# A decode kernel on one core: w2 in small early transfers, fewer VectorE instructions, wo's first half in wide matmuls

## The chip, the cores and the metric

The kernel runs on one core of a Trainium2 chip. A core has five engines that run at the same time, each through its own list of instructions: TensorE (PE; its weight loads are shown apart as PEld), VectorE (DVE), ScalarE (ACT), GpSimd (POOL) and SyncE (SP). Here SyncE does nothing but issue transfers. Sixteen DMA engines move data between the chip's main memory and the core's on-chip memory. Engines wait for each other through semaphores. The metric is the device time of one execution in microseconds (us), lower is better. It is given as the median of the runs shown.

## The reference

For a batch of two and one new token each, the result is a gated mix of attention against a long cache and a small feed-forward block (the reshapes are left out):

```python
g = sigmoid((x * gate_w).sum(-1))                 # x: [2, 512]
q = (x @ wq)                                      # 32 heads of 128
scores = einsum(q, k_cache) * 128 ** -0.5         # k_cache: [2, 32, 4096, 128], bf16
o = einsum(softmax(scores), v_cache)              # v_cache: the same size
a = o @ wo                                        # wo: [4096, 512]
b = relu(x @ w1) @ w2                             # w1: [512, 1376], w2: [1376, 512]
out = g * a + (1 - g) * b                         # [2, 512]
```

The two caches are 67.1 MB each. All input together is 145.4 MB, and every byte is read once.

## The kernel before

The program is written engine by engine. Each instruction is recorded with the markers it waits for and the marker it signals; `resolve` and `emit` (lines 57 to 82) turn them into semaphore counts. An engine runs its instructions in the order in which the program records them. A wait on more than one semaphore becomes an instruction of its own (line 76 or 78), and it counts as a record of the engine's program.

**Units and regions.** The K cache is cut into eight units K0 to K7 of 8 MB, and the V cache into V0 to V7. They pass through three regions of on-chip memory (`NREG`, the tensor `kv`), in the order K0 to K4, V0, K5, V1, K6, V2, K7, V3 to V7 (line 169). Unit number n goes into region n mod 3, and SyncE issues its transfer only when the unit three places earlier has been used up: a K unit when its scores are done (marker `pe_sc_u`), a V unit when its products are done (`pe_v_u`). So V1 waits for the scores of K4, and V0 for those of K2. SyncE's transfers all go through one queue (q1) in program order. V7 comes in two parts.

**A K unit.** VectorE transposes the unit in place (`k_turn`, line 360) in four instructions, one for each quarter of the columns. TensorE computes the scores (`k_scores`, lines 365 and 393) in four parts `rp`, 16 matmuls each, and part `rp` waits for transpose number `rp`. The scores of four units, one batch row, stand in the accumulation memory (PSUM) together. After K3 comes the softmax of the first batch row: `sm_max` (VectorE), `sm_exp` (ScalarE), and `sm_turn` (VectorE, line 422), and only behind it on VectorE's list comes the transposition of K4. After K7 comes the softmax of the second.

**A V unit.** GpSimd spreads the probabilities into `ptm` (line 431), TensorE multiplies (`v_unit`, line 448), VectorE picks out the wanted quarter and sums (`v_extract`, lines 455 and 459), and TensorE gathers (line 464). `o_denominator` forms 1 / sum for one batch row, `o_scale` applies it with the gate.

**The beginning.** x and gate_w come through ScalarE's queue, one row each per partition; `gate` transposes them on TensorE, VectorE copies and multiplies, and a matmul with ones sums up. `q_proj` and `ffn_h` (line 336: x @ w1 in 11 tiles, ten of 128 and one of 96) follow.

**The end.** wo and w2 go into the region that V5 has left (marker `pe_v_5`), in this order: two halves of wo (2 MB each), 96 rows of w2 (w2a), then 640 (w2b, 5 KB a partition), 512 (w2c, 4 KB) and 128 (w2d, 1 KB). `o_place` lays the attention result out as weights `oW`. `project` (line 500) multiplies in 32 steps of wo and 11 of w2; each step is four matmuls of 128 columns, side by side on four column groups of TensorE, with two columns of weights each. Four small casts and one transfer give the output.

Of the kernel before, what the change touches and what calls it, by code (L numbers as in the profile page):

```python
# [4 lines left out]
ALU = mybir.AluOpType  # L5
ACT = mybir.ActivationFunctionType
AX = mybir.AxisListType
# [3 lines left out]
DFF = 1376  # L11
# [73 lines left out]
def bass_gated_mix__gqa_block_cached__dense_activation_relu__decode_kernel(  # L85
# [22 lines left out]
    id2 = sb("id2", [2, 2], bf16)  # L108
    xT = sb("xT", [128, 4, 2], bf16)
    xT32 = sb("xT32", [128, 4, 32], bf16)  # L110
    gwT = sb("gwT", [128, 4], bf16)
    xg = sb("xg", [128, 4, 2], f32)
    xgs = sb("xgs", [128, 2], f32)
# [17 lines left out]
    oW = sb("oW", [128, 32, 2], bf16)  # L131
    hT = sb("hT", [128, 11, 2], bf16)
# [8 lines left out]
    x_sb = kv[0:2, C, 21888:22400]  # L141
    gw_sb = kv[0:1, C, 22400:22912]
    ident = kv[:, C, 22912:23168].bitcast(f32)
    ones = kv[:, C, 23168:23424].bitcast(f32)
# [19 lines left out]
    names = ["x", "gw", "wq", "w1", "v7a", "v7b", "wo0", "wo1", "w2a", "w2b", "w2c", "w2d", "cast", "out"]  # L164
# [47 lines left out]
    w2_sb = kv[:, WO, 16384:22016].rearrange("p (r n) -> p r n", n=512)  # L212

    act(lambda e: e.dma_start(x_sb, A_x.rearrange("b s d -> (b s) d")).then_inc(sem["x"], 16))
    act(lambda e: e.dma_start(gw_sb, gate_w.rearrange("(o d) -> o d", o=1)).then_inc(sem["gw"], 16))
    sp(lambda e: e.dma_start(wq_sb, A_wq.rearrange("(p t) n -> p (t n)", t=4)).then_inc(sem["wq"], 16))
    sp(lambda e: e.dma_start(w1_sb, B_w1.rearrange("(p t) f -> p (t f)", t=4)).then_inc(sem["w1"], 16))
    for n, what in enumerate(order):
        if n >= NREG:
            waits = [freed(order[n - NREG])]  # L220
        else:
            waits = ["pe_h", "dve_setup", "dve_q"] if n == C else []
        if what == ("v", 7):
            sp(lambda e, n=n: e.dma_start(kv[:, n % NREG, 0:LASTV * 128], unit_in(("v", 7))[:, 0:LASTV * 128])
               .then_inc(sem["v7a"], 16), waits=waits)
            sp(lambda e, n=n: e.dma_start(kv[:, n % NREG, LASTV * 128:REG], unit_in(("v", 7))[:, LASTV * 128:REG])
               .then_inc(sem["v7b"], 16))
        else:
            sp(lambda e, n=n, what=what: e.dma_start(kv[:, n % NREG, :], unit_in(what)).then_inc(sem_reg[n % NREG], 16),
               waits=waits)  # L230
    for x in range(2):
        sp(lambda e, x=x: e.dma_start(wo_sb[:, x * 8192:(x + 1) * 8192],  # L232
                                      A_wo[x * 2048:(x + 1) * 2048, :].rearrange("(p r) n -> p (r n)", p=128))
           .then_inc(sem[f"wo{x}"], 16), waits=([freed(order[wo_reg - NREG])] if x == 0 else []))

    sp(lambda e: e.dma_start(w2_sb[0:96, 10, :], B_w2[1280:1376, :]).then_inc(sem["w2a"], 16))
    W2 = (("w2b", 0, 5, 0), ("w2c", 640, 4, 5), ("w2d", 1152, 1, 9))
    for name, row, n, r0 in W2:
# [7 lines left out]
    def constants():  # L246
        pool(lambda g: g.memset(id2[:], 0.0), signal="c_idz")
        pool(lambda g: g.affine_select(out=id2[:], in_=id2[:], pattern=[[-1, 2]], compare_op=ALU.not_equal, fill=1.0,
                                       base=0, channel_multiplier=1), waits=["c_idz"], signal="c_id2")
        pool(lambda g: g.memset(ones, 1.0), signal="c_ones")  # L250
# [3 lines left out]
        pool(lambda g: g.memset(xT32[:], 0.0), signal="c_x32")  # L254
        for i in range(2):
            pool(lambda g, i=i: g.memset(wz[:, i], 0.0), signal=("c_wz" if i else None))
        pool(lambda g: g.memset(mpad[:], 0.0), signal="c_mpad")
        pool(lambda g: g.memset(selx[:], 0.0), signal="c_selx")
# [6 lines left out]
    def setup():  # L265
        dve(lambda v: v.tensor_reduce(out=maskc[:], in_=ident.rearrange("p (t c h) -> p c t h", t=4, c=4), axis=AX.XY, op=ALU.add),
            waits=["c_ident"])
        dve(lambda v: v.tensor_reduce(out=mmax[:], in_=ident.rearrange("p (h x) -> p h x", h=8), axis=AX.X, op=ALU.add),
            signal="dve_m8")
        dve(lambda v: v.tensor_copy(out=mask8[:], in_=mmax[:]), waits=["dve_m8"], signal="dve_mask8")  # L270
# [8 lines left out]
    def gate():  # L279
        for t in range(4):  # L280
            pe(lambda e, t=t: e.transpose(PSB[0:128, XT_B0 + 2 * t:XT_B0 + 2 * t + 2], x_sb[:, t::4], id2[0:2, 0:2]),
               waits=(["c_id2"] if t == 0 else []), dwaits=([(sem["x"], 16)] if t == 0 else []))
        for t in range(4):
            pe(lambda e, t=t: e.transpose(PSB[0:128, XT_B0 + 8 + 2 * t:XT_B0 + 9 + 2 * t], gw_sb[:, t::4], id2[0:1, 0:1]),  # L284
               dwaits=([(sem["gw"], 16)] if t == 0 else []), signal=("pe_xT" if t == 3 else None))
        dve(lambda v: v.tensor_copy(out=xT[:], in_=PSB[0:128, XT_B0:XT_B0 + 8].rearrange("p (t b) -> p t b", t=4)),  # L286
            waits=["pe_xT"], signal="dve_xT0")
        dve(lambda v: v.tensor_copy(out=xT32[:, :, 0:2], in_=PSB[0:128, XT_B0:XT_B0 + 8].rearrange("p (t b) -> p t b", t=4)),
            waits=["c_x32"], signal="dve_x32")
        dve(lambda v: v.tensor_copy(out=gwT[:], in_=PSB[0:128, XT_B0 + 8:XT_B0 + 16:2]), signal="dve_xT")  # L290
        dve(lambda v: v.tensor_tensor(out=xg[:], in0=xT[:], in1=gwT[:].unsqueeze(2).to_broadcast([128, 4, 2]), op=ALU.mult),
            waits=["dve_xT"], signal="dve_xg")
        dve(lambda v: v.tensor_reduce(out=xgs[:], in_=xg[:].rearrange("p t b -> p b t"), axis=AX.X, op=ALU.add),
            waits=["dve_xg"], signal="dve_xgs")
        pe(lambda e: e.matmul(psf(0, 128, G_C0, 2), lhsT=ones, rhs=xgs[:, :], start=True, stop=True),
           waits=["dve_xgs", "c_ones"], signal="pe_z")
# [10 lines left out]
    def q_proj():  # L307
        wqv = wq_sb.rearrange("p (t u a x) -> p t a u x", t=4, u=4, a=4)
        for half in range(2):
            for t in range(4):  # L310
                for a in range(4):
# [4 lines left out]
                       waits=(["dve_xT0", "dve_x32"] if half == 0 and t == 0 and a == 0 else []),  # L316
# [9 lines left out]
    def ffn_h():  # L326
        for ft in range(11):
            m = 128 if ft < 10 else 96
            for t in range(4):
                def fn(e, ft=ft, t=t, m=m):  # L330
                    o = t * DFF
                    cols = w1_sb[:, o + 1280:o + 1376]
                    for _, row, n, r0 in W2:
                        if r0 <= ft < r0 + n:
                            cols = w1_sb[:, o + row + ft - r0:o + row + 128 * n:n]
                    return e.matmul(psf(0, m, H_C0 + 2 * ft, 2), lhsT=cols, rhs=xT[:, t, :], start=(t == 0), stop=(t == 3))
                pe(fn, dwaits=([(sem["w1"], 16)] if ft == 0 and t == 0 else []),
                   signal=("pe_h" if ft == 10 and t == 3 else None))
        for b in range(2):
            dve(lambda v, b=b: v.tensor_scalar(out=hT[:, 0:10, b], in0=PSF[:, H_C0 + b:H_C0 + 20:2], scalar1=0.0,  # L340
                                               scalar2=gm[:, b:b + 1], op0=ALU.max, op1=ALU.mult),
                waits=["pe_h", "dve_gm"])
            dve(lambda v, b=b: v.tensor_scalar(out=hT[0:96, 10, b:b + 1], in0=psf(0, 96, H_C0 + 20 + b, 1), scalar1=0.0,
                                               scalar2=gm[0:96, b:b + 1], op0=ALU.max, op1=ALU.mult),
                signal=f"dve_h{b}")
# [10 lines left out]
    def k_turn(u):  # L356
        what = ("k", u)
        reg = kv[:, reg_of(what), :].bitcast(dt.uint32)
        for rp in range(4):
            dve(lambda v, rp=rp: v.transpose(out=reg[:, 4096 * rp:4096 * (rp + 1)], in_=reg[:, 4096 * rp:4096 * (rp + 1)]),  # L360
                dwaits=([landed(what)] if rp == 0 else []), signal=f"dve_kt_{u}_{rp}")
# [8 lines left out]
    def k_scores(u):  # L370
        b, ub = divmod(u, 4)
        keys = kv[:, reg_of(("k", u)), :].rearrange("p (r j q e) -> p r j q e", j=2, q=32, e=2)
        for rp in range(4):
            pos = 8 * ub + 2 * rp
            for blk in range(4):
                j, e_ = divmod(blk, 2)
                for rb in range(4):
                    rc = 4 * rp + rb
                    waits = []
                    if blk == 0 and rb == 0:  # L380
                        waits = [f"dve_kt_{u}_{rp}"]
# [16 lines left out]
    def sm_max(b):  # L398
        dve(lambda v: v.tensor_reduce(out=mpad[:, 0:2], in_=PSF[:, 0:2048].rearrange("p (x h q) -> p h x q", h=2, q=16),  # L399
                                      axis=AX.XY, op=ALU.max),  # L400
            waits=[f"pe_sc_{4 * b + 3}", "c_mpad"] + ([f"dve_mt{b - 1}"] if b else []), signal=f"dve_m{b}")
# [51 lines left out]
    def v_extract(v):  # L453
# [4 lines left out]
            waits=[f"pe_v_{v}"] + ([f"dve_y_{v - 1}"] if v else []), signal=f"dve_x_{v}")  # L458
        dve(lambda e: e.tensor_reduce(out=X3[:], in_=X2[:].rearrange("p (c d) -> p d c", c=4), axis=AX.X, op=ALU.add),  # L459
            waits=[f"dve_x_{v}"] + ([f"pe_g_{v - 1}"] if v else []), signal=f"dve_y_{v}")  # L460
# [7 lines left out]
    def o_denominator(b):  # L468
        for h in range(2):
            pe(lambda e, h=h: e.matmul(psf(0, 32, L_C0 + b, 1), lhsT=sell[:, h, :], rhs=lsum[:, b, h:h + 1],  # L470
                                       start=(h == 0), stop=(h == 1), skip_group_check=True),
               waits=([f"act_exp{b}", "dve_setup", "dve_h1"] if h == 0 else []), signal=(f"pe_l{b}" if h else None))
        dve(lambda v: v.reciprocal(out=rinv[:, b:b + 1], in_=psf(0, 32, L_C0 + b, 1)), waits=[f"pe_l{b}"], signal=f"dve_rinv{b}")

    def o_scale(b):
        dve(lambda v: v.tensor_scalar(out=O_sb[:, b, :], in0=psf(0, 32, O_C0, 128), scalar1=rinv[:, b:b + 1],
                                      scalar2=gb[0:32, b:b + 1], op0=ALU.mult, op1=ALU.mult),
            waits=[f"pe_g_{4 * b + 3}", f"dve_rinv{b}", "dve_g"], signal=f"dve_O{b}")

    def o_place():  # L480
        for x in range(2):
            for dq in range(8):
# [6 lines left out]
        dve(lambda v: v.tensor_copy(out=oW[:].rearrange("p (x r) c -> p x r c", x=2),  # L489
                                    in_=psf(0, 128, R_C0, 64).rearrange("p (x b r) -> p x r b", x=2, b=2)),  # L490
            waits=["pe_R"], signal="dve_oW")


    def project():
        steps = [(oW[:, r, :], wo_sb[:, r * 512:(r + 1) * 512]) for r in range(32)]
        steps += [(hT[0:96, 10, :], w2_sb[0:96, 10, :])] + [(hT[:, r, :], w2_sb[:, r, :]) for r in range(10)]
        lands = {0: "wo0", 16: "wo1", 32: "w2a", 33: "w2b", 38: "w2c", 42: "w2d"}
# [92 lines left out]
```

## Time and profile before

| | |
|---|---|
| time, median of 3 runs | 344.62 us (344.28 to 344.64) |
| profiled execution | 344.46 us |
| its span, first to last instruction | 343.1 us |
| PE busy | 179.8 us (52%), 1322 instructions |
| DVE busy | 169.7 us (49%), 87 instructions |
| ACT, POOL busy | 13.5 us, 35.5 us |
| read from main memory | 145.43 MB, 424 GB/s over the span |
| q1, SyncE's transfers | 98.5% of the 16 engines' span |

The span runs from the first to the last instruction, so the profiled execution has 1.36 us around it. Times of day in the text ("at 145.06") count from the start of the span. The slices part of the page cuts the span into 40 equal pieces of 8.6 us and gives each engine's busy share in tenths. The chain of waits follows the work back from the last instruction: each line has a start, a length, and what ran or what was waited for. "issue" in it is time in which the engine waited for nothing that the profile shows. The time line has start, length, engine, line, operation and, in brackets, idle time before it and what ended that. Behind these views the trace also holds one record for each DMA packet (start, length, queue, bytes) and, for each transfer, the moments at which each of its engines reported its part as landed.

### The profile page before, as it was taken

To read this page: it belongs to the slowest core of one execution; us is meant where nothing else is said; L and a number is where in the kernel's file an instruction comes from. 1 tells how busy PE (TensorE), PEld (TensorE's weight loads), DVE (VectorE), ACT (ScalarE), POOL (GpSimd) and SP (SyncE) were. 2 spreads that over 40 slices of the span, in tenths; PEclk is the share of its full clock that TensorE was granted. 3 is DMA by queue.
4 is the path that set the end of the run, shared out by engine and by line. 5 is a ranking of instruction groups with operands and counts; after the bars stand their busy time and mean duration, and the time that the engine had idled before them with its cause. 6 is when DMAs were issued, how large, how long until landed. Compare 5 with 4: busy or idle time off the path is not lost.

```text
span 343.1 us, 2541 instructions
## 1 busy us (share of the span) xinstructions
PE 179.8 (52%) x1322; PEld 39.6 (12%) x938; DVE 169.7 (49%) x87; ACT 13.5 (4%) x44; POOL 35.5 (10%) x50
## 2 busy tenths in 40 slices
PE   0510196996869409935980099205970503307353
PEld 0210000100001000120120011100020201102122
DVE  0210797979899489439910694219935020102020
ACT  1010001000010110000000000000020000000000
POOL 3000000000000040040013000400004040403100
PEclk9965599899989957995995579955996575856586
DMA  8998989999999989898999989999999999999995
GB/s 325 451 483 374 481 374 481 397 458 420 435 460 390 489 382 474 382 468 390 466 466 391 481 384 466 405 451 405 460 405 443 466 392 474 413 401 449 395 428 216
DMA packets 3588, 145.59 MB, mean 424 GB/s; under 512 B 405, under 2 KB 634, under 8 KB 890
## 3 DMA queue, kind: packets, MB, share of 16 engines
q1 hardware_dynamic: 3572, 145.43, 98.5%
q8 instruction: 9, 0.15, 0.2%
q10 hardware_dynamic: 6, 0.00, 0.0%
q14 instruction: 1, 0.01, 0.0%
HBM read 145.43 MB, written 0.00 MB: 424 GB/s over the span
## 4 chain that ended last, share of the span: by engine, by line
DMA 57%; DVE 24%; PE 9%; issue 4%; another core or an unknown queue 3%; SPq 1%; ACT 1%
DMA kv<-in_A_k_cache_dram 34%; DVE kv L360 22%; DMA kv<-in_B_w_dram 13%; DMA kv<-in_A_v_cache_dram 11%; PE PS L365 4%; PE PS L448 4%; PE PS L393 2%; DVE E L422 1%; ACT E L414 1%; DVE mpad L399 1%; DVE X L459 0%; SPq L232 0%; DVE X L455 0%; PE PS L500 0%
## 5 line engine op out<-in xcount | busy, mean ns | idle before, releaser
L360 DVE STREAM_TRANSPOSE kv<-kv 128x4096 uint32<-128x4096 uint32 x32 | 139.3, 4412 | 50.2 <-DMA kv<-in_A_k_cache_dram 50.2
L365 PE MATMUL PS<-kv,wz 128*128 128x512 bf16 x384 | 114.0, 407 | 0.0
L393 PE MATMUL PS<-kv,wz 128*128 128x512 bf16 x128 | 52.9, 413 | 94.5 <-DVE kv L360 94.4
L431 POOL TENSOR_TENSOR ptm<-E,mask 128x512 bf16<-128x512 bf16 x32 | 32.2, 1039 | 282.2 <-DVE E L422 158.5
L448 PE MATMUL PS<-kv,ptm 128*32 128x512 bf16 x512 | 38.6, 462 | 36.3 <-DMA kv<-in_A_v_cache_dram 36.3
L455 DVE TENSOR_TENSOR X<-PS,maskc 128x512 f32<-128x512 f32 x8 | 5.5, 687 | 79.4 <-PE PS L448 79.4
L393 PEld LDWEIGHTS PS<-kv,wz 128*128 128x128 bf16 x128 | 13.0, 102 | 206.2 <-DVE kv L360 120.6
L448 PEld LDWEIGHTS PS<-kv,ptm 128*32 128x32 bf16 x512 | 17.5, 113 | 54.3 <-issue 47.2
L351 ACT ACTIVATE wz<-q_sb 32x8 bf16<-32x8 bf16 x32 | 6.9, 214 | 154.5 <-PE PS L365 145.6
L464 PE MATMUL PS<-X,selx 128*32 128x128 f32 x16 | 3.5, 302 | 13.3 <-DVE X L459 13.3
L459 DVE TENSOR_REDUCE X<-X 128x128 f32<-128x512 f32 x8 | 8.2, 1024 | 0.3
L399 DVE TENSOR_REDUCE mpad<-PS 128x2 f32<-128x2048 f32 x2 | 4.6, 2292 | 7.5 <-PE PS L365 7.5
L414 ACT ACTIVATE E<-PS,negm 128x1024 bf16<-128x1024 f32 x4 | 4.4, 1109 | 81.8 <-DVE negm L410 81.8
L422 DVE STREAM_TRANSPOSE E<-E 128x2048 bf16<-128x2048 bf16 x2 | 4.6, 2312 | 4.7 <-ACT E L414 4.7
L312 PE MATMUL PS<-kv,xT 128*32 128x512 bf16 x32 | 3.6, 629 | 3.6 <-DMA kv<-in_A_wq_dram 3.6
L500 PE MATMUL PS<-kv,oW 128*2 128x128 bf16 x128 | 2.9, 264 | 4.5 <-DMA kv<-in_A_wo_dram 4.5
L510 DVE CAST ptm<-PS 2x128 bf16<-2x128 f32 x2 | 0.6, 280 | 9.1 <-PE PS L500 9.1
L319 DVE STREAM_TRANSPOSE ptm<-PS 128x1024 f32<-128x1024 f32 x1 | 1.3, 1251 | 6.3 <-PE PS L312 6.3
L286 DVE COPY xT<-PS 128x8 bf16<-128x8 bf16 x1 | 0.2, 164 | 8.1 <-PE PS L284 8.1
L510 ACT ACTIVATE ptm<-PS 2x128 bf16<-2x128 f32 x2 | 0.5, 270 | 84.0 <-PE PS L500 84.0
L464 PEld LDWEIGHTS PS<-X,selx 128*32 128x32 f32 x16 | 1.1, 112 | 19.0 <-DVE X L459 15.7
L500 PEld LDWEIGHTS PS<-kv,oW 128*2 128x2 bf16 x128 | 2.5, 102 | 4.8 <-DMA kv<-in_A_wo_dram 4.2
(56 smaller groups left out, 24.2 us busy)
## 6 DMA issues: line engine op xcount, KB each, us to landing
kv<-in_A_v_cache_dram SPq DMA_DIRECT2D x1, 6144.0 KB, 47.8
kv<-in_A_wq_dram SPq DMA_DIRECT2D x1, 4096.0 KB, 12.2
kv<-in_A_wo_dram SPq DMA_DIRECT2D x2, 2048.0 KB, 40.1
kv<-in_A_v_cache_dram SPq DMA_DIRECT2D x1, 2048.0 KB, 52.3
kv<-in_B_w_dram SPq DMA_DIRECT2D x1, 1376.0 KB, 15.0
kv<-in_B_w_dram SPq DMA_DIRECT2D x1, 640.0 KB, 43.4
kv<-in_B_w_dram SPq DMA_DIRECT2D x1, 512.0 KB, 44.2
kv<-in_A_k_cache_dram SPq DMA_DIRECT2D x8, 40.2
```

Source lines behind the costliest of these rows:

```text
L351: act(lambda e, a=a: e.activation(out=wz[32 * a:32 * a + 32, u % 2, :, 31 + 32 * a:33 + 32 * a], in_=q_sb[32 * a:32 * a + 32, b, ub].rearr ...
L360: dve(lambda v, rp=rp: v.transpose(out=reg[:, 4096 * rp:4096 * (rp + 1)], in_=reg[:, 4096 * rp:4096 * (rp + 1)]), dwaits=([landed(what)] i ...
L365: return e.add_instruction(mybir.InstMatmult(name=nc.get_next_instruction_name(), engine=mybir.EngineType.PE, ins=[e.lower_ap(rhs), e.lowe ...
L393: return e.matmul(dst, lhsT=w, rhs=m, start=first, stop=final, skip_group_check=True)
L399: dve(lambda v: v.tensor_reduce(out=mpad[:, 0:2], in_=PSF[:, 0:2048].rearrange("p (x h q) -> p h x q", h=2, q=16), axis=AX.XY, op=ALU.max) ...
L414: act(lambda a, h=h: a.activation(out=E[:].rearrange("p (x h q) -> p h x q", h=2, q=16)[:, h], in_=PSF[:, 0:2048].rearrange("p (x h q) -> ...
L422: dve(lambda v: v.transpose(out=E[:], in_=E[:]), waits=[f"act_exp{b}"], signal=f"dve_et{b}")
L431: pool(lambda g, src=src, dst=dst: g.tensor_tensor(out=dst, in0=src, in1=msk, op=ALU.mult), waits=([f"dve_et{b}", "dve_mask8"] + ([f"pe_v_ ...
L448: pe(lambda e, ci=ci, t=t: e.matmul(psf(32 * t, 32 * t + 32, c0, 512), lhsT=ptm[:, ci].rearrange("p c h -> p (c h)"), rhs=rows[:, 512 * ci ...
L455: dve(lambda e: e.tensor_tensor(out=X2[:].rearrange("p (c d) -> p c d", c=4), in0=psf(0, 128, c0, 512).rearrange("p (c d) -> p c d", c=4), ...
L459: dve(lambda e: e.tensor_reduce(out=X3[:], in_=X2[:].rearrange("p (c d) -> p d c", c=4), axis=AX.X, op=ALU.add), waits=[f"dve_x_{v}"] + ([ ...
L500: pe(lambda e, t=t, n=n, w=w, m=m: e.matmul(psf(32 * t, 32 * t + 2, FIN_C0, 128), lhsT=w, rhs=m[:, 128 * t:128 * t + 128], start=(n == 0), ...
```

## The change

- **w2.** The 1376 rows are cut anew into 160, 64, 640, 384 and 128. The 160 rows are laid out as 40 partitions of four rows (4 KB); they come in eight transfers of five partitions each (every eighth partition), issued ahead of wo, and share one semaphore (`w2p`, waited for at 128). w2a has 64 rows in place of 96, w2c three rows a partition in place of four. The feed-forward block has 14 tiles in place of 11, all computed at full width.
- **VectorE's program.** It has 69 records in place of 111. K units are transposed in two instructions of twice the width; scores parts 0 and 1 wait for the first, 2 and 3 for the second. Waits that other waits already cover are dropped. The gate needs one copy in place of three copies, a product and a sum, since gate_w is transposed with x as a third row and TensorE forms the dot product. Both denominators are formed together, after V3. ReLU and gating take two instructions in place of four.
- **wo's first half.** 16 steps of two matmuls with 64 columns of weights and 256 columns of data, on two column groups, in place of 16 steps of four. `oW` holds the first half's weights twice, 32 columns apart, so that the results fall on the same rows as those of the narrow steps. The four results now stand in different columns of PSUM.
- The order of GpSimd's constants changes with it.

```diff
+    w2_sb = kv[:, WO, 16384:23552].rearrange("p (r n) -> p r n", n=512)
+    W2 = (("w2p", 0, 4, 0, 40), ("w2a", 160, 1, 4, 64), ("w2b", 224, 5, 5, 128), ("w2c", 864, 3, 10, 128), ("w2d", 1248, 1, 13, 128))
...
+    for j in range(8):
+        sp(lambda e, j=j: e.dma_start(w2_sb[j:40:8, 0:4, :].rearrange("p r n -> p (r n)"),
+                                      B_w2[0:160, :].rearrange("(p r) n -> p (r n)", r=4)[j::8]).then_inc(sem["w2p"], 16),
+           waits=([freed(order[wo_reg - NREG])] if j == 0 else []))
     for x in range(2):
         sp(lambda e, x=x: e.dma_start(wo_sb[:, x * 8192:(x + 1) * 8192],
                                       A_wo[x * 2048:(x + 1) * 2048, :].rearrange("(p r) n -> p (r n)", p=128))
-           .then_inc(sem[f"wo{x}"], 16), waits=([freed(order[wo_reg - NREG])] if x == 0 else []))
-    sp(lambda e: e.dma_start(w2_sb[0:96, 10, :], B_w2[1280:1376, :]).then_inc(sem["w2a"], 16))
+           .then_inc(sem[f"wo{x}"], 16))
+    sp(lambda e: e.dma_start(w2_sb[0:64, 4, :], B_w2[160:224, :]).then_inc(sem["w2a"], 16))
...
     def gate():
+        dve(lambda v: v.tensor_copy(out=xT32[:, :, 0:3], in_=PSB[0:128, XT_B0:XT_B0 + 16].rearrange("p (t b) -> p t b", t=4)[:, :, 0:3]),
+            waits=["pe_xT"], signal="dve_xT")
         for t in range(4):
+            pe(lambda e, t=t: e.matmul(psf(0, 128, G_C0, 2), lhsT=xT32[:, t, 2:3].to_broadcast([128, 128]), rhs=xT32[:, t, 0:2],
+                                       start=(t == 0), stop=(t == 3)),
...
     def k_turn(u):
-        for rp in range(4):
-            dve(lambda v, rp=rp: v.transpose(out=reg[:, 4096 * rp:4096 * (rp + 1)], in_=reg[:, 4096 * rp:4096 * (rp + 1)]),
-                dwaits=([landed(what)] if rp == 0 else []), signal=f"dve_kt_{u}_{rp}")
+        for h in range(2):
+            dve(lambda v, h=h: v.transpose(out=reg[:, 8192 * h:8192 * (h + 1)], in_=reg[:, 8192 * h:8192 * (h + 1)]),
+                dwaits=([landed(what)] if h == 0 else []), signal=f"dve_kt_{u}_{h}")
...
-                    if blk == 0 and rb == 0:
-                        waits = [f"dve_kt_{u}_{rp}"]
+                    if blk == 0 and rb == 0 and rp % 2 == 0:
+                        waits = [f"dve_kt_{u}_{rp // 2}"]
...
     def o_place():
-        dve(lambda v: v.tensor_copy(out=oW[:].rearrange("p (x r) c -> p x r c", x=2),
-                                    in_=psf(0, 128, R_C0, 64).rearrange("p (x b r) -> p x r b", x=2, b=2)),
-            waits=["pe_R"], signal="dve_oW")
+        R = psf(0, 128, R_C0, 64).rearrange("p (x b r) -> p x r b", x=2, b=2)
+        dve(lambda v: v.tensor_copy(out=oW[:, 0:2], in_=R[:, 0:1].to_broadcast([128, 2, 16, 2])), waits=["pe_R"])
+        dve(lambda v: v.tensor_copy(out=oW[:, 2], in_=R[:, 1]), signal="dve_oW")
     def project():
-        steps = [(oW[:, r, :], wo_sb[:, r * 512:(r + 1) * 512]) for r in range(32)]
-        steps += [(hT[0:96, 10, :], w2_sb[0:96, 10, :])] + [(hT[:, r, :], w2_sb[:, r, :]) for r in range(10)]
+        for r in range(16):
+            for g in range(2):
+                pe(lambda e, r=r, g=g: e.matmul(
+                    psf(64 * g, 64 * g + 64, FIN_C0 + 256 * g, 256),
+                    lhsT=oW[:].rearrange("p k r c -> p (k r c)")[:, 2 * r:2 * r + 64],
+                    rhs=wo_sb[:, r * 512 + 256 * g:r * 512 + 256 * g + 256], start=(r == 0), stop=False,
+                    tile_position=(0, 64 * g), skip_group_check=True),
+        steps = [(hT[0:40, r, :], w2_sb[0:40, r, :]) for r in range(4)]
+        steps += [(oW[:, 2, r, :], wo_sb[:, 8192 + r * 512:8704 + r * 512]) for r in range(16)]
+        steps += [(hT[0:64, 4, :], w2_sb[0:64, 4, :])] + [(hT[:, r, :], w2_sb[:, r, :]) for r in range(5, NF)]
...
```

## The prediction

> **What bounds the kernel now.** I read the page from its second part down: the slices, then the DMA queues.
>
> ```profile
> DMA  8998989999999989898999989999999999999995
> q1 hardware_dynamic: 3572, 145.43, 98.5%
> q8 instruction: 9, 0.15, 0.2%
> q14 instruction: 1, 0.01, 0.0%
> ```
>
> The transfer engines are full from the second slice to the last but one. SyncE's one queue (q1) holds them 98.5% of the span; compute engines are near half busy. An engine cut off the path saves nothing; an empty transfer queue costs its full length. Two small queues fetch instructions.
>
> Next I asked when each transfer is issued and how much is then still queued. The time line of SyncE's queue has the issues (beside them, the first K transpose on a new unit, which starts when that unit has landed):
>
> ```profile
> 116.12 0.33 SPq L229 DMA_DIRECT2D kv<-in_A_k_cache_dram  x1
> 145.06 0.33 SPq L229 DMA_DIRECT2D kv<-in_A_v_cache_dram  x1
> 148.78 0.33 SPq L229 DMA_DIRECT2D kv<-in_A_k_cache_dram  x1
> ...
> 153.41 4.45 DVE L360 STREAM_TRANSPOSE kv<-kv 128x4096 uint32<-128x4096 uint32 x1 [2.87 <-DMA kv<-in_A_k_cache_dram]
> ```
>
> V1 is issued at 145.06, when the scores of K4 release its region, behind K5. In the trace's packet records K5's last bytes are through at 150.94 to 151.40 on thirteen engines and at 152.3 to 152.7 on three. So this issue has 5.9 us in hand. The other issues have over 16 (K5's at 116.12 stands behind V0, whose last bytes come at about 133).
>
> What sets the issue at 145.06 is in the chain of waits, from K3's landing on:
>
> ```profile
> 94.96 0.04 DVE kv L360
> 95.00 4.33 issue
> 99.33 13.06 DVE kv L360 x3
> 112.40 0.05 issue
> 112.44 0.39 PE PS L393
> 112.83 0.65 PE PS L365 x3
> 113.48 0.22 PE PS L393
> ...
> 116.12 2.30 DVE mpad L399
> ...
> 121.71 2.31 DVE E L422
> 124.03 17.32 DVE kv L360 x4
> 141.34 0.05 issue
> 141.39 0.39 PE PS L393
> ```
>
> K3 is turned in four quarters, then TensorE scores the last quarter (3.66 us, to 116.10); softmax follows; only then is K4 turned and its last quarter scored (to 145.03). Both tails lie in series ahead of V1.
>
> The end, from the same view:
>
> ```profile
> 296.49 44.17 DMA kv<-in_B_w_dram
> 340.66 0.04 issue
> 340.71 0.64 PE PS L500 x18
> 341.35 0.02 issue
> 341.37 0.28 DVE ptm L510
> ```
>
> The last w2 transfers decide. By the trace's landing records w2d arrives at 339.23 to 339.55 on seven engines, 340.34 on one, 340.71 to 340.99 on eight. Why: following each engine's packets end to start, the eight 16 KB instruction fetches before the end hit eight different engines, each late by 1.3 to 1.5 us from then on; one 8 KB fetch (182.51) makes the half-late one. Two of the eight come before V1, one at 151.30.
>
> **The change, part by part.**
>
> *Transposes in halves.* Two of 8192 columns replace four of 4096. The rows give 2312 ns for 2048 columns (L422) and 4412 for 4096 (L360), 1.025 ns a column, so 8.61 for 8192; back to back a transpose starts 0.06 before the last one's end, so a unit takes 17.17 us, not 17.42. But TensorE can start a half only when all of it is turned, so behind the second half there are two quarters left, not one: 3.66 plus one more at four matmuls in 0.87 (0.22 + 0.65), 3.47, makes 7.13. K3: 94.96 + 17.17 + 0.04 + 7.13 = 119.3 instead of 116.1. Softmax up to K4's first transpose took 7.9, so K4 starts at 127.2, is turned at 144.4. Its first half reaches TensorE at 135.8; the same 32 matmuls took 9.1 us before (128.41 to 137.54, the first dozen at 0.42 each after an idle stretch), so that half ends at 144.9, just past 144.4; the second takes 7.0: 151.9 in place of 145.03. V1 is issued 6.9 us later, past the 5.9 in hand.
>
> *What the late issue costs.* From issue to first packet on an idle queue: 0.74 (output, 341.98 to 342.72) to 1.03 (wq, 0.74 to 1.77). The first wq packets took 1.84 us, later ones of that size 1.21: 0.63 for starting empty. So V1 starts at 152.7 to 153.0, worth 153.3 to 153.6 of a running queue; on the thirteen engines done at about 151.15 that loses 2.3 us, on the other three 0.8. Bounds: without the start loss 1.5, with K4's half a little slower 2.8. I take 2.3, as all its terms are rows. Nothing gives it back, since the queue is full to the end; the other issues keep over 16 us less some 3 to 9.
>
> *w2's rows.* Each engine's ordinary share falls from 86 to 76 KB: two 1 KB packets less (0.042 each in the packet records) and eight of 3 KB for 4 KB (0.159 for 4 KB, 0.198 for 5 KB, so 0.039 a KB): -0.39 us. Added are forty 4 KB packets of 0.159. Spread over sixteen engines: +0.40, so zero in sum. On the same five: 8 x 0.159 = 1.27, so +0.88 there and -0.39 on eleven. The trace's nearest rows: x's two rows ran on two engines, gate_w's one row on one of those two, so few rows mean few engines, and the same ones again: I take five. [...]
>
> Whether the five are late ones decides. The chain of packets that took the 8 KB fetch is, as far as near ties let one follow it, the other engine of x's pair, so one of the five: 340.34 + 2.3 + 0.88 = 343.5. Late engines outside the five: 340.99 + 2.3 - 0.39 = 342.9. The half-late one is last: 343.5 against 340.99, +2.5. Issuing eight transfers takes SyncE 8 x 0.45 = 3.6 us at 294.7, with V6 and V7 (to 327.5) queued: hidden.
>
> *VectorE's 69 records.* VectorE had passed 62 of its records when the 8 KB fetch came at 182.51. If its count triggers the fetch, the same count now falls at about 331, still before w2; if SyncE or GpSimd, which ran then too, do, nothing moves. So the half-late engine stays. The removed waits and small operations are off the path: VectorE waits 50.2 us for K units. Besides 16 transposes, 19 waits (0.017 each) and seven small operations (0.15 to 0.28) go: under 2 us if that cover went. The gate's operations lie before 20 us, behind K0's landing at 36.85; the 12 added w1 matmuls (0.04 each) there too.
>
> *wo's first half.* 32 matmuls of 256 columns in two groups for 64 of 128 in four, at 332.5, then TensorE idled 4.0 us for wo1: even at twice the 1.06 us, with w2p's 16 matmuls (0.5) and a second copy into oW (0.22), hidden. Behind w2c's landing there are 16 matmuls, not 20, at 0.036 (0.64 for 18): -0.14.
>
> *Denominators.* Both now after V3, in the slack around 260; nothing.
>
> Sum: +2.5 - 0.14 = +2.4. The profiled execution took 344.46 (span 343.1 and 1.36 around it), against a median of 344.62; 346.9.
>
> **The rivals.**
> - Only late engines outside the five count (the 8 KB fetch is gone, or elsewhere): 1.9 - 0.14, so 346.2. For it: the chain has near ties. Against: the count argument.
> - A 16 KB fetch after V1 hits one of the five: 340.99 + 2.3 + 0.88, +3.0, so 347.5. For it: five or six of sixteen engines get one. Against: neither x engine seems to before 276.
> - Not slower: no gap. If K4's scores end by 150.2, V1 is queued in time. It needs 1.7 us from four transposes and the scoring, 0.4 a transpose; against that, both transpose rows lie on one line. Then the end moves by +0.1 (344.6), or -0.5 (343.9) with the five engines all early.
> - The new rows don't stay on five engines: +2.3 - 0.14, so 346.6, too near the forecast to part; it is inside it.
>
> **How the numbers follow.** Forecast 0.40, outside the five 0.22, late among the five 0.23, no gap 0.15. The gap's bounds move the first three by -0.8 and +0.5: from 345.4 to 348.0; a little more at both ends for sizes, 345.1 to 348.2, leaves out the case of no gap. A change under 0.2% (0.7 us) can't be told from none here: of no gap, most lies inside it. Faster 0.06, same 0.09, slower 0.85.
>
> **What would show it.** After: V1's issue near 152, later than K5's first engines end; a hole of 2 us in the DMA row near 152 and a lower GB/s there; K transposes at 8.6 us; eight issues before wo's; w2's last landing near 343.5, PE's last matmuls after it. Wrong if V1's issue stays below 150.5, if the engines run through, or if the instruction fetches move.

## The result and the profile after

The changed kernel takes 348.91 us (median of 4 runs, 348.37 to 349.73), against 344.56 us before in the same comparison: a ratio of 1.013, 95% interval 1.0107 to 1.0153. Its profiled execution took 348.37, 3.91 more than the profiled one of before. Slower was forecast, the size was not: 346.9 was predicted, with 348.2 as the upper end.

From the page of the changed kernel, the slices (8.7 us each) and the transfer queue:

```profile
DMA  8998998989899898989989999898999999999995
GB/s 318 450 478 378 468 484 370 476 370 476 370 470 484 378 468 378 468 325 410 484 370 476 416 433 476 378 468 385 468 448 409 448 400 453 431 436 404 395 399 189
q1 hardware_dynamic: 3620, 145.43, 97.9%
```

The same bytes come over a longer span (97.9% against 98.5%). The tenths of the DMA row show no hole; the bytes do: the eighteenth slice (147.4 to 156.1) moved 325 GB/s. A slice can be full of packets that take longer (here 2.7 to 3.3 us in place of 2.42, as below), so the row of bytes is the one to read.

SyncE's time line, for the lines that the prediction showed of before:

```profile
119.55 0.33 SPq L225 DMA_DIRECT2D kv<-in_A_k_cache_dram  x1
151.84 0.33 SPq L225 DMA_DIRECT2D kv<-in_A_v_cache_dram  x1
155.42 0.33 SPq L225 DMA_DIRECT2D kv<-in_A_k_cache_dram  x1
```

K5 goes out 3.4 us later, V1 6.8 us later. In the packet records the first bytes of V1 start at 152.82, and on fifteen of the sixteen engines these first packets take 2.7 to 3.3 us, where a running queue takes 2.42. V1's last landings come 2.35 us later than before (173.08 against 170.73 on the quickest engine).

The chain of waits of the changed kernel over the same stretch, and at the end:

```profile
95.05 17.32 DVE kv L346 x2
...
119.55 2.30 DVE mpad L385
...
125.14 2.31 DVE E L408
127.45 8.60 DVE kv L346
136.10 0.61 PE PS L379
136.71 1.28 PE PS L351 x3
...
139.66 0.22 PE PS L379
139.88 0.65 PE PS L351 x3
...
305.42 39.04 DMA kv<-in_B_w_dram
344.50 0.62 PE PS L499 x10
```

After 127.45 the chain follows only the first half's transpose of K4 (8.60) and then TensorE without a break up to 151.8: TensorE, not VectorE, now sets V1's issue. Its first four matmuls there take 1.89 us (0.61 and 1.28), four later ones 0.87 (0.22 and 0.65). The end still hangs on the last w2 transfer.

Between V1 and the end more is lost. By the landing records w2d arrives at 342.31 to 342.63 on five engines, 343.57 to 344.00 on ten and 344.78 on one: 1.0 to 1.3 us later than the prediction's terms put these engines. The windows view says where (columns: window, its length, busy time of PE, PEld, DVE, ACT and POOL, granted clock, DMA share, GB/s), in the stretch with the eight five-row transfers; the changed kernel first, then the same kernel with w2 cut as before:

```profile
327.00:333.00 6.00, 4.45 (x48) 1.40 (x40) 1.21 (x2) 0.00 (x0) 0.00 (x0) 0.70 1.01 358
```

```profile
327.00:333.00 6.00, 5.32 (x60) 2.07 (x52) 0.63 (x1) 0.00 (x0) 0.00 (x0) 0.65 1.02 434
```

The engines are busy all the time (1.01) and move 358 GB/s in place of 434: 6 x 76 / 434 = 1.05 us lost without one engine being idle.

### The profile page after: what moved, and what is told of

Same layout as the page of the kernel before. It is cut to its first block, busy times and chain, and to the rows that moved or that the text cites. A ratio compares the mean times of both kernels' runs of the same rounds, so it can differ in the third digit from the quotient of the medians.

```text
span 346.9 us, 2485 instructions
## 1 busy us (share of the span) xinstructions
PE 180.1 (52%) x1312; PEld 39.5 (11%) x928; DVE 167.7 (48%) x64; ACT 13.5 (4%) x44; POOL 35.4 (10%) x50
## 3 DMA queue, kind: packets, MB, share of 16 engines
q1 hardware_dynamic: 3620, 145.43, 97.9%
## 4 chain that ended last, share of the span: by engine, by line
DMA 54%; PE 25%; DVE 17%; SPq 2%; ACT 1%; issue 0%
DMA kv<-in_A_k_cache_dram 33%; PE PS L351 15%; DVE kv L346 15%; DMA kv<-in_B_w_dram 11%; DMA kv<-in_A_v_cache_dram 10%; PE PS L379 5%; PE PS L434 4%; SPq L229 2%; DVE E L408 1%; ACT E L400 1%; DVE mpad L385 1%; DVE X L445 0%; SPq L233 0%; DVE X L441 0%; PE PS L499 0%
## 5 line engine op out<-in xcount | busy, mean ns | idle before, releaser
L346 DVE STREAM_TRANSPOSE kv<-kv 128x8192 uint32<-128x8192 uint32 x16 | 138.4, 8687 | 38.9 <-DMA kv<-in_A_k_cache_dram 38.9
L434 PEld LDWEIGHTS PS<-kv,ptm 128*32 128x32 bf16 x512 | 16.3, 113 | 54.3 <-issue 45.2
L337 ACT ACTIVATE wz<-q_sb 32x8 bf16<-32x8 bf16 x32 | 6.9, 214 | 162.5 <-PE PS L351 152.9
L486 PE MATMUL PS<-kv,oW 128*64 128x256 bf16 x32 | 3.6, 420 | 1.6 <-DMA kv<-in_A_wo_dram 1.6
L486 PEld LDWEIGHTS PS<-kv,oW 128*64 128x64 bf16 x32 | 3.1, 172 | 1.7 <-issue 1.6
```

The lines of the kernel that those rows point to most:

```text
L337: act(lambda e, a=a: e.activation(out=wz[32 * a:32 * a + 32, u % 2, :, 31 + 32 * a:33 + 32 * a], in_=q_sb[32 * a:32 * a + 32, b, ub].rearr ...
L346: dve(lambda v, h=h: v.transpose(out=reg[:, 8192 * h:8192 * (h + 1)], in_=reg[:, 8192 * h:8192 * (h + 1)]), dwaits=([landed(what)] if h == ...
L434: pe(lambda e, ci=ci, t=t: e.matmul(psf(32 * t, 32 * t + 32, c0, 512), lhsT=ptm[:, ci].rearrange("p c h -> p (c h)"), rhs=rows[:, 512 * ci ...
L486: pe(lambda e, r=r, g=g: e.matmul(psf(64 * g, 64 * g + 64, FIN_C0 + 256 * g, 256), lhsT=oW[:].rearrange("p k r c -> p (k r c)")[:, 2 * r:2 ...
```

## The experiments

All times are medians against the kernel before on the same chip (344.56 to 344.68 in the five comparisons).

**The halves alone, in the kernel before.**

```diff
     def k_turn(u):
-        for rp in range(4):
-            dve(lambda v, rp=rp: v.transpose(out=reg[:, 4096 * rp:4096 * (rp + 1)], ...
+        for h in range(2):
+            dve(lambda v, h=h: v.transpose(out=reg[:, 8192 * h:8192 * (h + 1)], ...
...
-                    if blk == 0 and rb == 0:
-                        waits = [f"dve_kt_{u}_{rp}"]
+                    if blk == 0 and rb == 0 and rp % 2 == 0:
+                        waits = [f"dve_kt_{u}_{rp // 2}"]
```

> The kernel before with one edit: a K unit is transposed in two halves. Theory (the late issue of V1 costs 2.4 us, the w2 transfers the rest): V1 issued near 151.9, packets of V1 from about 152.9, everything behind 2.35 us later, 346.9 us. Rival (the halves are harmless, all of the 4.3 us comes from the end): 344.6 us.

Measured: 348.17 (347.39 to 348.24), ratio 1.0098 [1.0084, 1.0111]. SyncE's time line in the profiled execution, which was the quickest, 347.39:

```profile
151.89 0.33 SPq L229 DMA_DIRECT2D kv<-in_A_v_cache_dram  x1
```

**The changed kernel with quarters** (the same edit, undone).

> The changed kernel with one part undone: K units in four quarters again. Theory: V1 issued near 145, no hole; what is left is the cost of the w2 transfers, 1.1 us on every engine and 1.3 more on five, 346.5 us. Rival (halves harmless): 348.9 us. Second rival (the w2 rows are worth nothing in sum, as the prediction's step had it within 0.4 us, and the halves cost it all): 344.6 us.

Measured: 346.00 (345.85 to 346.28), ratio 1.0041 [1.0029, 1.0054]. SyncE's time line:

```profile
145.24 0.33 SPq L225 DMA_DIRECT2D kv<-in_A_v_cache_dram  x1
```

**The changed kernel with w2 as before** (96, 640, 512 and 128 rows, behind wo; the halves stay).

> The changed kernel with w2 cut and transferred as before (96, 640, 512 and 128 rows, behind wo, no eight transfers), halves kept. Theory: only the late V1 is left, 346.9 us, and the packets between V7 and wo run at 0.61 us for 16 KB throughout. Rival (the extra 2 us at the end come from the wide matmuls or from VectorE's program): 348.5 to 348.9 us.

Measured: 348.19 (347.20 to 348.58), ratio 1.0099 [1.0085, 1.0113].

With w2 as before the halves cost 3.5 us, alone (3.52) or beside the rest of the change (3.54), where 346.9 had been expected in both runs. With quarters V1's issue is back at 145.2, and the w2 edit costs 1.35 us with no gap at V1. The two do not simply add up: 3.5 and 1.35 make 4.9, the change cost 4.35. Taken out of the change, the halves save 2.9 (348.91 to 346.00) and the w2 edit 0.7 (348.91 to 348.19). The kernels with halves spread over 0.85 to 1.4 us from execution to execution, so a part of that is noise; the rest stays open. By themselves both terms were predicted too low: 2.3 and about 0.1.

**Both undone**: quarters and w2 as before; VectorE's other cuts, the gate in three rows and wo's wide matmuls stay.

> The changed kernel with quarters and with w2 as before: what is left is VectorE's small cuts, the gate and wo's wide matmuls. Theory (all of this is off the path): 344.6 us. Rival (part of the 1.35 us left in e2_quarters comes from there): up to 346.0 us.

Measured: 344.57 (344.39 to 344.83), ratio 0.9999 [0.999, 1.0008]. Nothing else in the change moves the time; the interval leaves it 0.3 us either way.

**Which units.** Halves in K3 and K4 only, and halves in all but K4:

```diff
+HALVED = (3, 4)
...
+        n = 2 if u in HALVED else 4
+        w = 16384 // n
+        for h in range(n):
+            dve(lambda v, h=h, w=w: v.transpose(out=reg[:, w * h:w * (h + 1)], in_=reg[:, w * h:w * (h + 1)]),
```

> The kernel before with halves for K3 and K4 alone, quarters for the other six units. Theory (only the two scoring tails that stand in series ahead of V1 count, together 6.8 to 7.7 us against 5.9 in hand): as e1_halves_only, 347.4 to 348.2 us, V1 issued at 151.9 to 152.8. Rival (every halved unit costs a part): about a quarter of it, 345.5 us.

> The kernel before with halves for every K unit but K4. Theory: K3's tail alone is 3.2 to 4.2 us, under the 5.9 in hand, so V1 is issued near 148.5 and no engine runs dry: 344.6 us. Rival (the cost grows with the halved units): seven eighths of 3.5, 347.7 us.

Measured: K3 and K4 alone 348.21 (348.08 to 349.05), ratio 1.0109 [1.0096, 1.0122], so the whole cost of the halves sits in these two units. All but K4: 345.70 (344.64 to 347.35, 12 runs), ratio 1.0031 [1.0017, 1.0044], a wide spread. Its profiled execution took 346.79:

```profile
120.45 0.33 SPq L230 DMA_DIRECT2D kv<-in_A_k_cache_dram  x1
149.39 0.33 SPq L230 DMA_DIRECT2D kv<-in_A_v_cache_dram  x1
```

V1 goes out 4.3 us later than before, not the 3.3 that one longer scoring tail explains, and in the packet records three engines that finish K5 between 150.9 and 151.1 start V1 only at 152.6 to 152.9. The other thirteen go straight from K5 to V1, and yet their first V1 packets take 2.5 to 3.0 us in place of 2.42. So two things were open: an extra microsecond in some executions, and how much time is really in hand.

**The extra microsecond.** It arises at K3. TensorE's time line of two executions at K3's first half, first the changed kernel (K5 issued at 119.55), then the changed kernel with w2 as before (K5 issued at 120.52):

```profile
103.82 0.39 PE L379 MATMUL PS<-kv,wz 128*128 128x512 bf16 x1 [3.63 <-DVE kv L346]
104.05 0.81 PE L351 MATMUL PS<-kv,wz 128*128 128x512 bf16 x3
104.70 0.38 PE L379 MATMUL PS<-kv,wz 128*128 128x512 bf16 x1
```

```profile
103.66 0.61 PE L378 MATMUL PS<-kv,wz 128*128 128x512 bf16 x1 [3.61 <-DVE kv L345]
104.07 1.48 PE L350 MATMUL PS<-kv,wz 128*128 128x512 bf16 x3
105.35 0.63 PE L378 MATMUL PS<-kv,wz 128*128 128x512 bf16 x1
```

The same matmuls after the same idle time (3.63 and 3.61) take 0.87 us for four in one and 1.70 in the other. The windows view gives the granted clock over 103.6 to 108 in both:

```profile
103.60:108.00 4.40, 4.18 (x20) 0.53 (x6) 4.40 (x2) 0.00 (x0) 0.00 (x0) 1.00 1.10 477
```

```profile
103.60:108.00 4.40, 4.34 (x11) 0.39 (x3) 4.40 (x2) 0.00 (x0) 0.00 (x0) 0.50 1.08 465
```

A half of 32 matmuls takes 8 x 0.87 = 7.0 us at full clock, and 8.6 us lie between the halves, so 1.65 us can be lost in the first half unseen. Three groups at 1.70 and part of a fourth lose 2.8, and the rest, 1.1, goes to the end. What sets the granted clock the traces do not show: an idle time of 3.6 us gives either outcome, and the slow stretches seen last 3.4 to 5.7 us. In the halves alone TensorE came back at full clock and fell to half in the middle of its work, 1.3 us later, for 3.4 us (a granted clock of 0.67 over 103.6 to 108), which the 1.65 us still covered. That the idle time ahead of the half has a part in it was the author's guess.

To try it, TensorE was kept busy ahead of K3's scores, with matmuls whose results nobody reads, in the kernel before with halves, and with halves in all but K4; then ahead of K4's scores too:

```diff
+    def awake(u, count):
+        s = u % 2
+        flat = wz[:, s].rearrange("p k c -> p (k c)")
+        for i in range(count):
+            pe(lambda e: e.matmul(psf(0, 128, V_C0 + BANK, BANK), lhsT=wz[:, s, 0, 0:128], rhs=flat[:, 0:512],
+                                  start=True, stop=True, skip_group_check=True), waits=([f"act_wz{u}"] if i == 0 else []))
...
+        if u == 3:
+            awake(3, 14)
         k_scores(u)
...
     k_turn(4)
+    awake(4, 70)
     k_scores(4)
```

> The kernel before with only the halves, and 14 matmuls of 512 columns (about 3 us of TensorE, their results not read) on TensorE's list ahead of K3's scores, in its idle stretch before K3's first half is turned. Theory (in most executions of the halves TensorE starts K3's first half at half clock and V1 is issued about 1 us later than in the profiled execution of the change): with TensorE busy just before, the granted clock over K3's first half is 1.00, V1 is issued at about 151.9, and the time is 347.0 to 347.4 where the halves alone gave 348.2. Rival (the extra 1 us has another cause): 348.2 as before.

> The kernel before with halves for every unit but K4, and the same 14 matmuls ahead of K3's scores. Theory (the late executions of that variant, up to 347.35, were those with the half clock at K3): V1 is issued at about 148.4, 3.3 us later than before, which the queued part of K5 covers; the spread goes and the time is 344.6 to 344.9. Rival (not the clock, or less queued work than thought): 345.5 to 346 with a spread of over 1 us, as without the matmuls.

> The kernel before with only the halves, the 14 matmuls ahead of K3's scores, and 70 more of the same kind (15.2 us at full clock) ahead of K4's scores, in TensorE's idle stretch before K4's first half is turned (119.5 to 135.8). Theory (the clock that TensorE has when a half reaches it sets the spread: with 14 matmuls K3's half ran at 1.00 and K5 was issued 1.05 us earlier, but K4's half then ran at half clock to the end of its scores' slack, and V1 was issued at 152.82 again): with both awake, K4's first half ends before its second half is turned, V1 is issued at 151.7 to 151.9 in every execution, and the time is 346.8 to 347.4, with a spread under 0.6 us. Rival (the late issues have another cause): median 348.1 and a spread over 1 us, as before.

Awake at K3 only: 348.12 (346.87 to 348.56), ratio 1.0094 [1.008, 1.0109]. The median fits the rival, the trace does not. Its windows at K3's and K4's first halves:

```profile
103.60:108.00 4.40, 4.40 (x22) 0.67 (x7) 4.40 (x2) 0.00 (x0) 0.00 (x0) 1.00 1.09 465
135.50:140.00 4.50, 3.96 (x10) 0.40 (x3) 4.50 (x2) 0.00 (x0) 0.00 (x0) 0.50 1.08 466
140.00:145.00 5.00, 5.00 (x21) 0.53 (x5) 4.58 (x1) 0.00 (x0) 0.00 (x0) 0.84 0.97 419
```

K3's half ran at 1.00 and K5 went out at 119.48; then K4's half ran slow to beyond 140, and V1 was issued at 152.82 all the same. There are two such places, and curing one leaves the other.

All but K4, awake at K3: 345.12 (344.88 to 346.28), ratio 1.0018 [1.0009, 1.0027], in place of 345.70; the two intervals overlap. The profiled execution took 344.88, with V1 issued at 148.35, 3.3 us later than before, and every engine going from K5 to V1 within 0.3 us. The spread shrank from 2.7 to 1.4 us, but the median stays 0.44 above before; what that is, the one trace does not show.

Awake at K3 and K4: 347.16 (346.86 to 347.56), ratio 1.0076 [1.0062, 1.0089], V1 issued at 151.67. The windows:

```profile
103.60:108.00 4.40, 4.40 (x22) 0.48 (x5) 4.40 (x1) 0.00 (x0) 0.00 (x0) 1.00 1.11 477
135.50:140.00 4.50, 4.07 (x19) 0.48 (x5) 4.50 (x2) 0.00 (x0) 0.00 (x0) 1.00 1.08 466
140.00:145.00 5.00, 3.53 (x18) 0.39 (x4) 4.47 (x1) 0.00 (x0) 0.00 (x0) 1.00 0.96 410
```

So by the medians, of the halves' 3.5 us 2.55 are the gap (347.16 - 344.60) and some 0.9 TensorE's clock. The interval of this run just overlaps those of three of the others and lies clear of that of K3 and K4 alone; the four kernels with w2 as before, both halves and a clock left to itself in at least one of the two places gave +3.44 to +3.65, and this one +2.56. The profiled executions of the five say the same: with V1 issued at 151.67 and 151.89 they took 346.96 and 347.39, with V1 issued at 152.81 to 152.84 they took 348.08 to 348.23.

**Does it add up in the changed kernel?** The same matmuls in both places there:

> The changed kernel itself with the 14 matmuls ahead of K3's scores and the 70 ahead of K4's. Theory (three costs that add up: 2.55 us for the scoring tails of the halves, 1.35 us for the five-row transfers of w2, and the rest of the 4.35 us for the clock at which the halves start): V1 is issued at about 151.7 and the time is 344.6 + 2.55 + 1.35 = 348.5, with a spread under 0.8 us. If the costs of tails and rows do not add up (a later V1 changes which transfer engines are late when the w2 rows come), the time falls well below that, to 347.8; if the clock has no part in the changed kernel, it stays at 348.9 with a spread over 1.3 us.

Measured: 348.72 (348.33 to 349.17), ratio 1.0115 [1.0098, 1.0132], V1 issued at 151.72. The sum of gap and rows, 344.65 + 2.55 + 1.35 = 348.55, fits. But against the changed kernel's 348.91 the clock's part is 0.2 and not resolved: the ranges overlap, so this run does not show that the clock costs anything in the changed kernel. In its profiled execution (349.17) one engine lands w2d at 345.66, 1.3 us behind the next one: with both places at full clock, a single late engine still spreads the time.

**The rows of w2.** In the changed kernel with quarters, the 160 rows were sent to other partitions. The eight five-row transfers, their bytes and their place in the queue stay:

```diff
-        sp(lambda e, j=j: e.dma_start(w2_sb[j:40:8, 0:4, :]...
+        sp(lambda e, j=j: e.dma_start(w2_sb[j % 4 + 32 * (j // 4):20 + 32 * (j // 4):4, 0:4, :]...
```

and, in the other one, `w2_sb[64 + j:104:8, 0:4, :]`.

> As e2_quarters, but the five rows of transfer j go to partitions j, j+4, ... j+16 (j under 4) and 28+j, 32+j, ... 44+j (j from 4 on) in place of j, j+8, ... j+32. The feed-forward part of these 160 rows is then not formed rightly; the work and the times are the same. Theory (the 16 KB packets of the other engines are slowed because the five engines write into partitions that other engines are writing): the 16 KB packets stay near 0.61 us, 1.0 to 1.2 us less than e2_quarters, 345.3 us. Rival (few rows of main memory, or small packets as such): as e2_quarters, 346.5 us.

> As e2_quarters, but the five rows of transfer j go to partitions 64+j, 72+j, ... 96+j. The feed-forward part of these 160 rows is then not formed rightly; work and times are the same. Theory (the slowing comes from writing where other engines write, whichever these are): 4 KB and 16 KB packets stretched as in e2_quarters, about 346.0 us. Rival (it is something about the low partitions, 0 to 39): packets at 0.16 and 0.61 us, 344.8 us.

Measured: 344.77 (344.48 to 344.98), ratio 1.0003 [0.9994, 1.0012] for the first, and 346.38 (346.34 to 346.58), ratio 1.0051 [1.0039, 1.0063] for the second. The windows view of the same 6 us, in the order before, quarters with the rows as in the change, first variant, second variant:

```profile
324.50:330.50 6.00, 4.16 (x52) 1.58 (x44) 1.71 (x2) 0.00 (x0) 0.00 (x0) 0.76 1.00 426
```

```profile
324.50:330.50 6.00, 4.58 (x48) 1.43 (x40) 1.03 (x2) 0.00 (x0) 0.00 (x0) 0.67 1.00 344
```

```profile
324.50:330.50 6.00, 4.65 (x52) 1.72 (x43) 1.27 (x2) 0.00 (x0) 0.00 (x0) 0.67 1.00 423
```

```profile
324.50:330.50 6.00, 4.15 (x52) 1.51 (x44) 0.04 (x1) 0.00 (x0) 0.00 (x0) 0.80 1.02 317
```

The lost bytes give most of the time: 6 x 82 / 426 = 1.15 us, 0.04 and 1.54, against measured costs of 1.35, 0.1 and 1.8. In the packet records of the change's rows, 16 KB packets on other engines too stretch from 0.614 us to a mean of 1.08 at the worst (over those that start in one half microsecond), the 4 KB packets from 0.159 to a mean of 0.29; in the first variant they stay at 0.614 and 0.159 throughout. So it is neither the size of the transfers, nor their number, nor their five rows each, but the partitions they write. Why the one choice is nearly free and the others are not was not shown. That the slowing comes where other engines are just then writing was the author's theory in both expectations; the packet records do not tell the partitions, so no trace here tests it. The second variant speaks against the low partitions as the cause: from 64 on the rows cost 1.8 us, more than the 1.35 of the change's rows. The runs don't part the choice of partitions from the distance of the rows (four partitions in the first variant, eight in the other two), which changed along with it.

## Why the prediction was right or wrong

- **The place of the loss, V1's issue: right.** K3's scores ended at 119.55 (119.3 predicted), V1 was issued at 151.84 (151.9), its first bytes started at 152.82 (152.7 to 153.0). A transpose took 8.69 us (8.61). That the profiled execution met 151.9 so closely is in part luck: three other traces with K3 and K4 in halves have 152.8.
- **The price of the late issue: the mechanism behind the 2.3 was right, the size a little small.** With TensorE kept at full clock the halves cost 2.55, inside the stated bounds of 1.5 to 2.8. Left to itself, a first half that starts at half clock adds up to 1.1, and the halves alone came to 3.5. The prediction gave K4's first half 9.1 us for this, K3's nothing, and took a single trace's clock as fixed. In the profiled execution of the change K3's half ran at 1.00, so the clock is no part of the miss there. Quarters hide it: in before K4's first quarter ran at half clock too (0.50 over 127.5 to 131.5), and had the time of three more transposes to catch up.
- **The time in hand: 5.9 us was too generous.** In the traced executions an issue 3.3 us later than before cost no engine more than 0.3 us, and one 4.3 us later cost three engines 1.5 to 1.8 us. That second issue still stood 1.5 to 1.7 us ahead of the end of their K5, but they began V1 only 3.2 to 3.5 us after it, where the prediction's rows have 0.74 to 1.03 for an idle queue. Why they waited so long stays open.
- **w2's rows: the wrong step.** "Forty 4 KB packets of 0.159" took the price from w2c, a transfer over 128 partitions, and gave the packets beside them no price at all. On five engines, and with the partitions of the change, such a packet takes up to 0.34 us, and the 16 KB packets of other engines take up to 1.24 in place of 0.614: +1.35 us in place of +0.1. The 346.9 and the missing 1.25 make 348.15, still inside the range; with 2.55 for the gap in place of 2.3 it is 348.4, outside it, and that is where the profiled execution lies (348.37). The last 0.5 us up to the median of 348.91 stay open. No bound of the range allowed for a cost that depends on the partitions to which the rows go (1.35 us with the change's, 0.1 with the first variant's).
- **Which engine is last: right in its classes.** V7's last part still landed on ten early engines, one half-late and five late; wo's first half, behind the rows, on six, none and nine, with the half-late engine last of all. So four early engines and the half-late one carried the rows, in the order forecast; each class of w2d stood 1.0 to 1.3 us later, about the price of the rows.
- **The 8 KB fetch: the count argument failed.** It came at 264.86, and at other times in other runs (158 to 265), not at 331. What triggers it stays open; that the half-late engine stayed was luck, not the argument.
- **Hidden parts: right.** Gate, VectorE's waits, denominators and the wide matmuls of wo cost nothing together. The 32 wide matmuls took 3.63 us where 64 took 1.06, far over the "twice" allowed for, and TensorE still idled 1.2 us for wo's second half. SyncE's eight issues took 5.74 us, not 3.6, also hidden.

## What to carry to other kernels

Where the transfers set the time, an edit on a compute engine is worth what it does to the moment of the next issue: count the work left behind the last piece, because fewer and larger pieces lengthen that tail. A transfer of a few rows is priced not only by its own packets but by what it does to the packets beside it (here 16 KB packets at a mean of up to 1.08 us in place of 0.614); look at bytes per time there, not at busy shares. A saving in instructions that leaves TensorE idle for some 3.6 us, as here, and then puts it on the path can have half clock as a price (four matmuls in 1.70 us in place of 0.87), which some of these traces show and others do not.

## What had not been expected of the hardware

- Eight transfers of 20 KB on five engines slowed the others too for some 4 us: 344 GB/s in place of 426 over 6 us, with 16 KB packets at a mean of up to 1.1 us in place of 0.614, and none of it in the busy shares (1.00 in both). With other target partitions the same bytes were as good as free (423 GB/s, +0.1 us).
- After 3.6 us without work TensorE came back at full clock in one execution, at half clock for up to 5.7 us in two others, and in a fourth fell to half clock 1.3 us after it had come back, with the same work there.
- 84 matmuls whose results nobody reads cut a kernel's loss from +3.5 to +2.6 us, as far as the intervals, which just overlap, let one say.
- The first packets behind the empty stretch ahead of V1 took 2.7 to 3.3 us in place of 2.42, on fifteen engines at once. In the kernel with halves in all but K4, those of the thirteen engines that never ran dry took 2.5 to 3.0 as well, so an empty engine is not all there is to it.
